# Seven products in place of eight for MLP2's gate and value, with its decoded weights staged through DRAM

## The chip, the cores and the metric

One core of a Trainium2 chip runs the kernel. The metric is the device time of one execution in microseconds, as the median of several runs. The core has a matrix engine (PE), whose weight loads the profile lists apart (PEld), a vector engine (DVE), an activation engine (ACT) and a general engine (POOL). SP issues most of the transfers; ACT can issue some too. On-chip memory is called SBUF, and PE writes its sums to PSUM.

## The reference

Three layers follow each other. The first is a chunked state-space attention over 4 x 8 x 768 tokens, whose output is reshaped to 3072 tokens of 256 numbers. The two others are the MLPs:

```
h = x @ w_in                                   # 256 -> 2048
g = where(h > 0, h, exp(min(h, 0)) - 1)
x = g @ w_out                                  # 2048 -> 256     (MLP1)
g = x @ w_gate                                 # 256 -> 1536
val = x @ w_val                                # 256 -> 1536
out = (g * (1 / (1 + exp(-g))) * val) @ w_out2 # 1536 -> 256     (MLP2)
```

All inputs are float32.

## The kernel before, in words

**Numbers.** PE multiplies in a short format (fp32r). So nearly every float32 operand is held as a high part and a low part: ACT copies the value into the short format (high), and DVE or POOL subtracts that from the value (low). One exact product is then three matmuls, high x high, low x high, high x low (`mm3`, line 547, which issues them at line 555).

**Blocks.** The 3072 tokens are six blocks of 512 (`BLOCKS`). MLP1 runs over 6 blocks x 16 slices `f` of 128 hidden numbers, MLP2 over 6 blocks x 12 slices. A pair (block, slice) is here called a slot. The loop at line 815 goes through 96 MLP1 slots and then 72 MLP2 slots. In each it issues the slot's input product, its activation, and the output product of the slot three back (`LAG`). The attention units of block b+1 are worked into the MLP1 slots of block b, at offsets written by hand (`OFF`, `OFF1`, `OFF8`), so block 5, the last, has none. Each engine runs what it is given in program order.

**MLP1's slot.** `m_a` is 6 matmuls into one of two banks `h`. ACT makes relu(-h) (line 577) and its exponential (line 582), DVE joins them with h (line 583, which frees the bank), `split` makes the high part on ACT (line 560) and the low part on POOL (line 561), and `m_c` is 6 matmuls (line 604). Block 0 has a cheaper form of `m_c` (line 596). `m_end` (line 610) writes the block's result to `x2`.

**MLP2's slot.** `s_a` (line 657) is 12 matmuls: for gate and for value, 2 halves of the 256 inputs x 3. ACT makes the sigmoid of the gate (line 671), DVE multiplies it by the gate (line 676) and by the value (line 677), both of which it reads from PSUM. `split` follows, on ACT and POOL. `s_c` (line 680) is 6 matmuls, 2 halves of the output x 3. So a slot has 18 matmuls of 128x512. `s_end` (line 692) copies a block's two outputs out, one on DVE (line 696) and one on ACT (line 698), and SP stores them (line 699). `s_x` (line 648) splits a block's `x2` into high and low (lines 653, 654).

**MLP2's weights.** They come as float64 words. `decode` (line 121) loads a piece (line 132), ACT makes a scaled copy of the upper words (line 138), and DVE makes three steps `d0`, `d1`, `d2` (lines 141, 144, 148). A slice has 768 columns: 256 gate, 256 value, 256 output. `load_w2` (line 618) takes them in pieces of 512 and 256, and `step_w2` (line 630) makes the steps one by one: three for every four slots of blocks 1 to 4 (`W2K`), which decodes 8 of the 12 slices into the buffer `w2e`, and two a slot in block 5, which decodes the other 4. `pair_w2` (line 638) makes the high part on ACT (line 642) and the low part on DVE (line 643), in block 5 for four slices and in the first slots of MLP2 for the rest. Then high and low stay in SBUF for all blocks.

**Other work that the prediction names.** In the attention, DVE's line 370 is a scan of 1024 columns, POOL's line 480 a product of 128 columns.

Of the kernel before, what the change touches and what calls it, by code (L numbers as in the profile page):

```python
# [67 lines left out]
def ssm_mlp_glu_kernel(ctx, tc, a, bcs, xbc, w1, w2, consts, out):  # L68
# [548 lines left out]

    def load_w2():

        f, j = parts[len(loaded)]  # L620
        if j == 0:
            V2[f] = w2e[:, f * 768:(f + 1) * 768] if f < NE else ph2["w2l"].tile([128, 768], F32, name=f"w2v{f}")
        v = V2[f]
        cs = slice(0, 512) if j == 0 else slice(512, 768)
        load, ex, steps = decode(w2.bitcast(U32)[f, :, 2 * cs.start:2 * cs.stop])
# [22 lines left out]
    def s_x(b):
        n = BLOCKS[b]
        pool = ph2["xs" if b % 2 == 0 else "w2h"]  # L650
        hi = pool.tile([128, 2, 512], F32R, tag="x2h", name="x2h")[:, :, :n]
        lo = pool.tile([128, 2, 512], F32R, tag="x2l", name="x2l")[:, :, :n]
        nc.scalar.activation(hi, x2[b], AF.Copy)
        nc.vector.tensor_tensor(lo, x2[b], hi.bitcast(F32), ALU.subtract)
        xs[b] = (hi, lo)

    def s_a(b, f):
        n = BLOCKS[b]
        res = []
        for nm in "gv":  # L660
            p = ph2["ps" if nm == "g" else "psv"].tile([128, 512], F32, tag="h" if nm == "g" else "v", name=nm, bufs=2 if nm == "g" else 3)[:, :n]
            wh, wl = W2[nm, f]
            mm3(p, [((wh[:, k], wl[:, k]), (xs[b][0][:, k], xs[b][1][:, k])) for k in range(2)], True, True)
            res.append(p)
        gps[b, f] = res

    def s_e1(b, f):
        n = BLOCKS[b]
        pg, pv = gps.pop((b, f))
        m = work.tile([128, 512], F32, tag="m", name="m2")[:, :n]  # L670
        nc.scalar.activation(m, pg, AF.Sigmoid)  # L671
        gt[b, f] = m, pg, pv

    def s_e1b(b, f):
        m, pg, pv = gt[b, f]
        nc.vector.tensor_tensor(m, m, pg, ALU.mult)  # L676
        nc.vector.tensor_tensor(m, m, pv, ALU.mult)  # L677
        gt[b, f] = m

    def s_c(b, f, half=None):  # L680
        n = BLOCKS[b]
        if f == 0:
            ops_[b] = [ph2["ps"].tile([128, 512], F32, tag=f"c{m}", name=f"o{m}")[:, :n] for m in range(2)]
        g = gt[b, f] if half == 0 else gt.pop((b, f))
        wh, wl = W2["o", f]
        for m in range(2):
            if half is not None and m != half:
                continue
            ms = slice(m * 128, (m + 1) * 128)
            mm3(ops_[b][m], [((wh[:, ms], wl[:, ms]), g)], f == 0, f == NF2 - 1)  # L690
# [222 lines left out]
```

## Time and profile before

| | us |
|---|---|
| median of 3 runs (632.03 to 632.95) | 632.71 |
| the profiled execution | 632.59 |
| its span, first to last instruction | 630.8 |

| engine | busy us | share of the span |
|---|---|---|
| PE | 616.5 | 98% |
| PEld | 490.3 | 78% |
| DVE | 369.1 | 59% |
| ACT | 316.4 | 50% |
| POOL | 317.8 | 50% |

The profiled execution is 1.8 us longer than its span, for what lies before the first and after the last instruction. Busy is the time in which at least one instruction of the engine ran; a matmul's 0.39 us overlaps the next one's, so PE's load is read from the distance of the starts. The granted TensorE clock is 1.000, full speed, over the whole span.

### The profile page before, as it was taken

The page shows a single profiled execution, that of the slowest core. Times are in us where ns is not written, and L with a number is a line of the kernel's source. Part 1 is how long each engine was busy: PE and PEld are TensorE (multiplying, and loading weights), DVE is VectorE, ACT ScalarE, POOL GpSimd, SP SyncE. Part 2 cuts the span into 40 slices and gives each one's busy share as a digit, 9 for nine tenths or more (in the row PEclk, how much of TensorE's full clock was granted, in tenths as well). Part 3 has the DMA queues.
Part 4 walks back from the last instruction along what each step waited for, and adds up shares of the span by engine and source line. Part 5 has one row for each costly group of instructions (what it writes and reads, how often), then busy time and mean ns, then how long its engine had stood idle before and what let it go on. Part 6 is the DMA issues. An engine that isn't in the chain of part 4 may idle for free.

```text
span 630.8 us, 9681 instructions
## 1 busy us (share of the span) xinstructions
PE 616.5 (98%) x3632; PEld 490.3 (78%) x3632; DVE 369.1 (59%) x574; ACT 316.4 (50%) x572; POOL 317.8 (50%) x269
## 2 busy tenths in 40 slices
PE   5899999999999999999999999999999999999997
PEld 4556667778888888778878888888888888888886
DVE  6898878998687767754664753433433343343332
ACT  1455667767677667657785533322323322332322
POOL 4443569998887878754553333233333322333332
PEclk9999999999999999999999999999999999999999
DMA  7588534444454454211300000000000000000000
GB/s 210 204 276 255 159 107 156 132 135 148 142 150 133 136 156 145 81 34 50 101 0 1 0 2 33 1 1 27 7 0 1 33 1 1 35 0 1 34 0 33
DMA packets 21014, 49.26 MB, mean 78 GB/s; under 512 B 3544, under 2 KB 5976, under 8 KB 20968
## 3 DMA queue, kind: packets, MB, share of 16 engines
q1 hardware_dynamic: 20664, 48.46, 24.5%
q8 instruction: 28, 0.46, 0.3%
q10 hardware_dynamic: 304, 0.19, 0.1%
q14 instruction: 18, 0.15, 0.1%
HBM read 45.40 MB, written 3.24 MB: 77 GB/s over the span
## 4 chain that ended last, share of the span: by engine, by line
PE 82%; DVE 4%; issue 1%; ACT 1%; POOL 1%; DMA 0%; SPq 0%; DVEq 0%
PE h L555 16%; PE o L555 16%; PE v L555 16%; PE g L555 16%; PE c L604 15%; PE cb L431 1%; PE y L508 1%; PE c L596 1%; DVE m L583 1%; PE y L504 1%; DVE zc L319 1%; DVE E L370 1%; DVE E L445 0%; POOL xb L392 0%; DVE wov L144 0%
## 5 line engine op out<-in xcount | busy, mean ns | idle before, releaser
L561 POOL TENSOR_TENSOR gl<-m,gh 128x512 fp32r<-128x512 f32 x152 | 204.8, 1348 | 248.9 <-ACT gh L560 248.9
L676 DVE TENSOR_TENSOR m<-m,g 128x512 f32<-128x512 f32 x72 | 49.5, 688 | 163.9 <-ACT m L671 163.9
L671 ACT ACTIVATE m<-g 128x512 f32<-128x512 f32 x72 | 43.1, 599 | 185.6 <-PE g L555 185.5
L583 DVE SCALAR_TENSOR_TENSOR m<-m,h 128x512 f32<-128x512 f32 x96 | 65.6, 683 | 60.1 <-ACT m L582 60.0
L560 ACT ACTIVATE gh<-m 128x512 fp32r<-128x512 f32 x152 | 94.9, 624 | 10.7 <-DVE m L583 9.7
L555 PE MATMUL h<-xh,wih 128*128 128x512 f32 x192 | 81.5, 424 | 2.3 <-DVE x L476 1.9
L577 ACT ACTIVATE m<-h 128x512 f32<-128x512 f32 x96 | 56.9, 592 | 49.1 <-PE h L555 45.9
L555 PE MATMUL h<-xh,wil 128*128 128x512 f32 x192 | 75.9, 395 | 0.0
L604 PE MATMUL c<-gh,woh 128*128 128x512 f32 x160 | 62.3, 390 | 0.0
L604 PE MATMUL c<-gh,wol 128*128 128x512 f32 x160 | 62.3, 389 | 0.0
L582 ACT ACTIVATE m<-m 128x512 f32<-128x512 f32 x96 | 59.8, 623 | 0.5
L555 PE MATMUL h<-xl,wih 128*128 128x512 f32 x192 | 59.8, 392 | 0.0
L555 PE MATMUL g<-x2h,w2h 128*128 128x512 f32 x144 | 56.0, 389 | 0.0
L555 PE MATMUL g<-x2h,w2l 128*128 128x512 f32 x144 | 56.0, 389 | 0.0
L555 PE MATMUL v<-x2h,w2h 128*128 128x512 f32 x144 | 56.0, 389 | 0.0
L555 PE MATMUL v<-x2h,w2l 128*128 128x512 f32 x144 | 56.0, 389 | 0.0
L555 PE MATMUL o<-gh,w2h 128*128 128x512 f32 x144 | 56.0, 389 | 0.0
L555 PE MATMUL o<-gh,w2l 128*128 128x512 f32 x144 | 56.0, 389 | 0.0
L555 PE MATMUL o<-gl,w2h 128*128 128x512 f32 x144 | 56.0, 389 | 0.0
L677 DVE TENSOR_TENSOR m<-m,v 128x512 f32<-128x512 f32 x72 | 49.5, 688 | 7.5
L604 PE MATMUL c<-gl,woh 128*128 128x512 f32 x160 | 50.9, 389 | 0.0
L555 PEld LDWEIGHTS h<-xh,wih 128*128 128x128 f32 x192 | 36.5, 190 | 15.4 <-DVE m L583 3.9
(144 smaller groups left out, 1076.2 us busy)
## 6 DMA issues: line engine op xcount, KB each, us to landing
abc<-ac SPq DMA_DIRECT2D x16, 512.0 KB
bcraw<-in_bcs SPq DMA_DIRECT2D x32, 256.0 KB
raw<-in_w SPq DMA_DIRECT2D x14, 512.0 KB
w2e<-in_w SPq DMA_DIRECT2D x14, 512.0 KB
xb<-in_xbc SPq DMA_DIRECT2D x18, 256.0 KB
raw<-in_w SPq DMA_DIRECT2D x12, 256.0 KB
out_y<-yo SPq DMA_DIRECT2D x12, 256.0 KB
x<-in_xbc SPq DMA_DIRECT2D x5, 256.0 KB
```

Of the source, the lines that this page charges most:

```text
L319: eng.tensor_tensor(u[z], u[raw], u[z].bitcast(F32), ALU.subtract)
L370: nc.vector.tensor_tensor_scan(u["E"].rearrange("p h q -> p (h q)"), u["abc"].rearrange("p h q -> p (h q)"), ident8.rearrange("p h q -> p ...
L555: nc.tensor.matmul(dst, lhsT=l, rhs=r, start=first and i == 0, stop=last and i == len(ops) - 1, **kw)
L560: nc.scalar.activation(hi, src, AF.Copy)
L561: lo_eng.tensor_tensor(lo, src, hi.bitcast(F32), ALU.subtract)
L577: nc.scalar.activation(m, h, AF.Relu, scale=-1.0)
L582: nc.scalar.activation(m, m, AF.Exp, scale=-1.0)
L583: nc.vector.scalar_tensor_tensor(m, m, -1.0, h, ALU.add, ALU.max)
L604: nc.tensor.matmul(cps[b][m], lhsT=w[:, m * 128:(m + 1) * 128], rhs=r, start=f == 0 and w is wh and r is gh, stop=f == NF1 - 1 and r is gl)
L671: nc.scalar.activation(m, pg, AF.Sigmoid)
L676: nc.vector.tensor_tensor(m, m, pg, ALU.mult)
L677: nc.vector.tensor_tensor(m, m, pv, ALU.mult)
```

## The change

**The product.** For one slice, the gate and value weights are a 2 x 2 arrangement (gate, value by the two halves of the inputs), and two neighbouring blocks give a 2 x 2 arrangement of `x2` (two halves of the inputs by two blocks). The product of the two takes eight products of 128x128 by 128x512. The change takes a form of Strassen's scheme with seven, over three pairs of blocks x 12 slices, 36 steps in all. It needs four sums of the weights (`w2_sums`, on POOL, 128 columns each), four differences of the inputs (`x_sum`, DVE for the first pair, POOL for the others), and sums of the products behind (`s_step`). A step has 7 x 3 matmuls for gate and value and 4 x 3 for the output (`s_o`), 33. The sigmoid and one multiplication become one `Silu` on ACT. PSUM has four banks `pa` to `pd` for the products, of which three take a second product on top of the first.

**The weights.** All 12 slices are decoded in whole pieces of 768 columns in blocks 2 to 4: 10 steps of DVE in block 2, 11 in block 3, 15 in block 4, none in blocks 1 and 5. Each slice is stored to DRAM by a transfer on ACT's queue, in one of three buffers by turns, and loaded again by SP when its turn comes: three slices in block 5, the others in the first pair's steps 0 to 8. There they get their sums on POOL (slice f at step f-3), their high parts on ACT and their low parts on DVE in two parts of 640 and 512 columns (step f-2).

**The order.** MLP1 no longer overlaps with MLP2's slots: step 0 begins behind slot 95, and holds the last three `m_c`. Steps have places (`a` to `d`, `o`) at which other work is hooked in.

The core of the diff:

```
-NHL = 4
+NHL = 3
...
-W2K = [0,0,1,2]
-W2N = 2
+W2K = [[0], [1,0,1,1,0,1,0,1,1,0,1,0,1,1,0,1], [1,0,1,1,0,1,1,0,1,1,0,1,1,0,1,1], [1,1,1,1]]
+NR = 3
+WS = 1152
+OPS = ["b11", "t2", "t3", "t1", "b21", "t4", "b22"]
...
     def load_w2():
...
+        f = len(loaded)
+        v, raw, e = w2e[:, f % NR * 768:][:, :768], w2e[:, NR * 768 + f % 2 * 1536:][:, :1536], w2e[:, NR * 768 + 3072:][:, :768]
+        load, ex, steps = decode(w2.bitcast(U32)[f], raw, e)
         load()
+        loaded.append(f)
+        def end():
+            steps[2](v)
+            spills.append([2, lambda: nc.scalar.dma_start(v2d[f], v)])
+        w2steps.extend([lambda: (ex(), steps[0](v)), lambda: steps[1](v), end])
...
+    def w2_load(f):
+        pool = ph2["w2l" if f < NHL or f % 2 else "w2h"]
+        v = V2[f] = pool.tile([128, WS], F32, tag="v2", name=f"v2_{f}")
+        nc.sync.dma_start(v[:, :768], v2d[f])
+    def w2_sums(f):
+        a11, a12, a22, s3, s1, s2, s4 = (V2[f][:, 128 * i:128 * i + 128] for i in (0, 1, 2, 5, 6, 7, 8))
+        nc.gpsimd.tensor_tensor(s1, s3, a22, ALU.add)
+        nc.gpsimd.tensor_tensor(s3, a11, s3, ALU.subtract)
+        nc.gpsimd.tensor_tensor(s2, s1, a11, ALU.subtract)
+        nc.gpsimd.tensor_tensor(s4, a12, s2, ALU.subtract)
+    cols = [slice(0, 640), slice(640, WS)]
...
+    def x_sum(p, nm, eng):
...
+        l, r = dict(t3=("b22", "b12"), t1=("b12", "b11"), t2=("b22", "t1"), t4=("b21", "t2"))[nm]
+        eng.tensor_tensor(x[nm], x[l], x[r], ALU.subtract)
...
+    def s_step(j, hooks):
+        p, f = divmod(j, NF2)
...
+        def g_split(j, i, m, eng):
+            hi, lo = [work.tile([128, 512], F32R, tag=f"g{z}", name=f"g{z}", bufs=LAG + 1) for z in "hl"]
+            nc.scalar.activation(hi, m, AF.Copy)
+            eng.tensor_tensor(lo, m, hi.bitcast(F32), ALU.subtract)
+            gt[j, i] = hi, lo
+        prod("a", 0, "b11", True)
+        prod("b", 7, "t2", True)
+        prod("d", 5, "t3", True)
+        prod("c", 6, "t1", True)
+        s1 = mtile("s1")
+        nc.scalar.activation(s1, ps["a"], AF.Copy)
+        if j:
+            g_split(j - 1, 1, V.pop(j - 1), nc.gpsimd)
...
+        nc.vector.tensor_tensor(u2, s1, ps["b"], ALU.add)
+        nc.vector.tensor_tensor(u3, u2, ps["d"], ALU.add)
+        nc.scalar.activation(s5, ps["c"], AF.Copy)
+        hook("a")
...
+        nc.vector.tensor_tensor(u3, u3, s5, ALU.add)
+        prod("a", 1, "b21", False)
+        prod("d", 2, "t4", False)
+        prod("c", 8, "b22", False)
+        m0 = mtile("m0")
+        nc.scalar.activation(m0, ps["a"], AF.Silu)
+        hook("b")
+        nc.vector.tensor_tensor(s1, u2, ps["d"], ALU.add)
+        nc.vector.tensor_tensor(u2, u2, ps["c"], ALU.add)
+        nc.vector.tensor_tensor(m0, m0, s1, ALU.mult)
+        m1 = mtile("m1")
+        nc.scalar.activation(m1, u2, AF.Silu)
+        g_split(j, 0, m0, nc.gpsimd)
+        hook("c")
+        nc.vector.tensor_tensor(m1, m1, u3, ALU.mult)
+        V[j] = m1
+        hook("o")
+        if j:
+            for i in range(2):
+                for m in range(2):
+                    s_o(j - 1, i, m)
...
+        if j == 3 * NF2 - 1:
+            g_split(j, 1, V.pop(j), nc.vector)
+            for i in range(2):
+                for m in range(2):
+                    s_o(j, i, m)
+                    s_end(p, i, m)
+        hook("d")
...
         for i in range(W2S, last_a):
-            at(late, i, step_w2, W2K[(i - BASE) % 4], NE)
-        for i in range(last_a + 1, last_a + 17):
-            at(late, i, step_w2, W2N, NF2)
+            at(late, i, step_w2, W2K[i // NF1 - 1][i % len(W2K[i // NF1 - 1])])
+        at(late, last_a, open_a)
...
+        hooks = {}
+        for f in range(NHL, NF2):
+            if f > NHL:
+                at(hooks, (f - 4, "d"), w2_load, f)
+            at(hooks, (f - 2, "a"), w2_hi, f, 0)
+            at(hooks, (f - 3, "a"), w2_sums, f)
+            at(hooks, (f - 2, "b"), w2_hi, f, 1)
+            at(hooks, (f - 2, "b"), w2_lo, f, 0)
+            at(hooks, (f - 2, "d"), w2_lo, f, 1)
+        for p in range(1, NB // 2):
+            e = p * NF2
+            for k, nm in enumerate(("t3", "t1", "t2", "t4")):
+                at(hooks, (e - 5 + k, "c"), x_sum, p, nm, nc.gpsimd)
+            for k, nm in enumerate(OPS):
+                i, h, l = [(e - 3, "b", "d"), (e - 2, "b", "d"), (e - 2, "c", "d"), (e - 1, "b", "d"), (e - 1, "b", "d"), (e - 1, "c", "d"), (e - 1, "c", "a")][k]
+                at(hooks, (i, h), x_hi, p, nm)
+                at(hooks, (i + (l == "a"), l), x_lo, p, nm, nc.gpsimd if nm == "t4" else nc.vector)
```

`x_hi` and `x_lo` make high and low parts of 512 columns, `w2_hi` and `w2_lo` those of the weights' parts `cols`. A block's two outputs are copied out as before, on DVE and ACT, in the second step of the next pair.

## Rows read from the trace of the kernel before

**Rows 1.** Busy time by stretch: us, then per engine busy us (instructions), clock, DMA.

```profile
88.90:144.70 55.80, 55.28 (x382) 43.86 (x382) 49.10 (x65) 41.03 (x79) 53.91 (x42) 1.00 0.44 137
144.70:195.30 50.60, 50.60 (x338) 41.08 (x337) 38.44 (x61) 35.37 (x68) 40.46 (x33) 1.00 0.46 142
195.30:245.80 50.50, 50.50 (x329) 40.86 (x328) 37.65 (x61) 35.27 (x68) 39.29 (x32) 1.00 0.47 141
245.80:293.90 48.10, 48.10 (x269) 38.73 (x268) 28.92 (x47) 32.47 (x63) 30.37 (x24) 1.00 0.18 63
293.90:341.70 47.80, 47.80 (x211) 39.09 (x210) 27.12 (x46) 34.20 (x63) 23.14 (x17) 1.00 0.17 50
341.70:626.90 285.20, 285.20 (x1260) 236.18 (x1258) 115.39 (x157) 91.92 (x158) 90.74 (x70) 1.00 0.03 10
```

**Rows 2.** The page's chain that ended last, shares of the span by engine.

```profile
PE 82%; DVE 4%; issue 1%; ACT 1%; POOL 1%; DMA 0%; SPq 0%; DVEq 0%
```

**Rows 3.** Timeline of PE in MLP2: start, duration, engine, line, operands; two slots' first matmuls.

```profile
500.58 0.39 PE L555 MATMUL g<-x2h,w2h 128*128 128x512 f32 x1
...
504.66 0.39 PE L555 MATMUL g<-x2h,w2h 128*128 128x512 f32 x1
```

**Rows 4.** Groups by line, 341.7 to 626.9 us: busy us, mean ns, idle before.

```profile
L561 POOL TENSOR_TENSOR gl<-m,gh 128x512 fp32r<-128x512 f32 x70 | 90.7, 1296 | 192.4 <-ACT gh L560 192.4
...
L677 DVE TENSOR_TENSOR m<-m,v 128x512 f32<-128x512 f32 x69 | 47.5, 688 | 7.2
L560 ACT ACTIVATE gh<-m 128x512 fp32r<-128x512 f32 x70 | 43.6, 624 | 1.0 <-DVE m L677 1.0
...
L671 ACT ACTIVATE m<-g 128x512 f32<-128x512 f32 x69 | 41.3, 599 | 180.9 <-PE g L555 180.8
```

**Rows 5.** Timeline of one MLP2 slot: from the gate's last matmuls to the multiplications.

```profile
615.73 0.62 PE L555 MATMUL g<-x2l,w2h 128*128 128x512 f32 x2
...
616.44 0.60 ACT L671 ACTIVATE m<-g 128x512 f32<-128x512 f32 x1 [2.96 <-PE g L555]
...
617.07 0.69 DVE L676 TENSOR_TENSOR m<-m,g 128x512 f32<-128x512 f32 x1 [2.60 <-ACT m L671]
...
617.86 0.69 DVE L677 TENSOR_TENSOR m<-m,v 128x512 f32<-128x512 f32 x1
```

**Rows 6.** Timeline of DVE and POOL where two instructions overlap, at two places.

```profile
310.06 2.11 POOL L561 TENSOR_TENSOR gl<-m,gh 128x512 fp32r<-128x512 f32 x1 [0.96 <-ACT gh L560]
310.06 0.95 DVE L643 TENSOR_TENSOR w2l<-w2e,w2h 128x768 fp32r<-128x768 f32 x1
...
348.42 1.30 POOL L561 TENSOR_TENSOR gl<-m,gh 128x512 fp32r<-128x512 f32 x1 [2.78 <-ACT gh L560]
...
349.19 1.34 DVE L643 TENSOR_TENSOR w2l<-w2e,w2h 128x768 fp32r<-128x768 f32 x1
```

**Rows 7.** Groups by line, 88.9 to 330 us: DVE's long scan, POOL's small product.

```profile
L370 DVE TENSOR_TENSOR_SCAN E<-abc,ident 128x1024 f32<-128x1024 f32 x15 | 34.9, 2324 | 0.0
...
L480 POOL TENSOR_TENSOR sbd<-x,con 128x128 f32<-128x128 f32 x15 | 7.4, 495 | 0.0
```

**Rows 8.** DVE's instructions on the weights' buffer alone: us, busy us (instructions), clock, DMA.

```profile
88.90:144.70 55.80, 11.69 (x12) 1.00 0.44 137
144.70:195.30 50.60, 6.49 (x12) 1.00 0.46 142
195.30:245.80 50.50, 6.13 (x12) 1.00 0.47 141
```

**Rows 9.** The chain in order of time: one attention unit's long input product.

```profile
166.75 1.58 PE h L555 x6
```

**Rows 10.** Issue of a transfer on ACT's queue; ACT's table load at MLP2's start.

```profile
0.74 0.58 ACTq L714 DMA_DIRECT2D w2e<-in_consts  x1
...
L671 ACT ACT_TABLE_LOAD  x1: 1283/1283/1283, 330.8 to 330.8; - x1
```

**Rows 11.** Timeline of the end: the last copy and the last stores' issue.

```profile
626.62 1.59 SPq L699 DMA_DIRECT2D out_y<-yo  x2
...
627.26 0.60 ACT L698 ACTIVATE yo<-o 128x512 f32<-128x512 f32 x1 [3.96 <-PE o L555]
```

More of the change, by code (lines that the diff above doesn't have):

```diff
@@ L46 @@
 EB = 1
-PW0 = 8
 WARM = 0
@@ L118, in ssm_mlp_glu_kernel, with decode @@
     top = low - H * R - NT // 16
-    def decode(src, raw=None):
+    def decode(src, raw=None, e=None):
         tot = src.shape[1] // 2
@@ L136, in ex @@
         def ex():
-            t["e"] = stg.tile([128, 512], F32, tag="e", name="e", bufs=EB)[:, :tot]
+            t["e"] = e if e is not None else stg.tile([128, 512], F32, tag="e", name="e", bufs=EB)[:, :tot]
             nc.scalar.activation(t["e"], t["hi"].bitcast(F32), AF.Copy, scale=REBIAS)
@@ L610, in m_end, with spill_w2, step_w2 @@
             nc.scalar.activation(x2[b][:, m, :], c[m], AF.Copy)
-    W2, V2, xs, gps, ops_ = {}, {}, {}, {}, {}
-    parts = [(f, j) for f in range(NF2) for j in range(2)]
-    loaded, w2steps = [], []
+    W2, V2, xs, ops_, V = {}, {}, {}, {}, {}
+    loaded, w2steps, spills = [], [], []
     def load_w2():
[L620 to L625, printed above, removed]
-        load()
-        loaded.append((f, j))
-        w2steps.extend([lambda: (ex(), steps[0](v[:, cs]))] + [lambda st=st: st(v[:, cs]) for st in steps[1:]])
-    def step_w2(n, upto):
+        f = len(loaded)
+        v, raw, e = w2e[:, f % NR * 768:][:, :768], w2e[:, NR * 768 + f % 2 * 1536:][:, :1536], w2e[:, NR * 768 + 3072:][:, :768]
+        load, ex, steps = decode(w2.bitcast(U32)[f], raw, e)
+        load()
+        loaded.append(f)
[3 more added lines that the diff above has]
+        w2steps.extend([lambda: (ex(), steps[0](v)), lambda: steps[1](v), end])
+    def spill_w2(now=False):
+        for z in list(spills):
+            z[0] -= 1
+            if now or z[0] <= 0:
+                z[1]()
+                spills.remove(z)
+    def step_w2(n):
+        spill_w2()
         for _ in range(n):
-            if len(loaded) < 2 * upto and len(w2steps) <= 3:
+            while len(loaded) < NF2 and len(w2steps) <= 3:
                 load_w2()
@@ L648, in s_x @@
[L648 to L681, printed above, removed]
-        if f == 0:
[L683 to L690, printed above, removed]
@@ new lines, in x_lo, with s_half, s_o @@
+    def x_lo(p, nm, eng):
+        hi, lo = xs[p, nm]
+        eng.tensor_tensor(lo, XT[p][nm], hi.bitcast(F32), ALU.subtract)
+    def s_half(j, i):
+        return (ident8.rearrange("p h q -> p (h q)"))[:, 512 * i:512 * i + 512]
+    def s_o(j, i, m):
+        p, f = divmod(j, NF2)
+        if f == 0:
+            ops_[p, i, m] = ph2["ps"].tile([128, 512], F32, tag="h" if i else f"c{m}", name=f"o{i}{m}", bufs=2 if i else None)
+        ms = slice(384 + m * 128, 384 + m * 128 + 128)
+        mm3(ops_[p, i, m], [([w[:, ms] for w in W2[f]], gt[j, i])], f == 0, f == NF2 - 1)
```

182 lines of the change are left out of this document (109 added, 73 removed).

## The prediction

> **What bounds the kernel now.** I read the busy time by stretch first, because shares of the whole span mix stages with different limits. PE is busy all through blocks 2 to 5 of MLP1 and through MLP2, and has 0.52 us without work in block 1 (55.28 of 55.80); in MLP2 DVE works 115 of 285 us, ACT 92, POOL 91 [rows 1]. The chain that ended last says the same: 82% of it is PE [rows 2]. But a busy PE may still be a slow one, so I take the distance of starts. One MLP2 slot follows the other after 504.66 - 500.58 = 4.08 us [rows 3], and a slot is 18 matmuls: 0.2267 us each. The whole stretch gives 285.2 / 1260 = 0.2263 us [rows 1]. So MLP2 is matmuls without a gap at the full clock, and only fewer matmuls make it shorter. In MLP1 DVE is the next engine: 88% of block 1, 76% and 75% of blocks 2 and 3, 60% of block 4 [rows 1].
>
> **Part 1, the matmuls.** A pair of slots has 36 matmuls now, a step 33, and the step has the same shapes. 36 steps x 3 x 0.2267 = **-24.5 us**. All of it lies on the path, since nothing else does. A step without waits is 33 x 0.2267 = 7.48 us; below, times count from its first matmul.
>
> **Part 2, what a step asks of the others.** DVE has 7 operations of 512 columns at 0.69 [rows 4] and about four handovers of 0.10 from one to a next that needs it (617.07 + 0.69 to 617.86 [rows 5]): 5.2 us. ACT has 6 at 0.60 to 0.62, 3.7 us; POOL two at 1.30, 2.6 us [rows 4]. All fit into 7.48. The one tight place is the second product into bank d: it may not start before DVE has read the first out of it (u3). A product's end is heard 0.48 us after its last matmul's start (that one starts at 615.73 + 0.23, ACT at 616.44 [rows 5]). So: a is ready at 0.45 + 0.48 = 0.93, ACT's copy ends at 1.53, u2 waits for b (1.61) and ends at 2.30, u3 runs 2.40 to 3.09. PE comes to d again after 15 matmuls, at 3.40: 0.31 us to spare. The other banks have more. The output matmuls of the step before start at 4.76 and need POOL's low part, made by 3.6, only at 6.57. Cost of a plain step: 0. The cover is that 0.31 us; anything that puts DVE further back than this PE feels at once.
>
> In the first pair the weights are made ready in the same steps. DVE gets low parts of 640 and 512 columns, 0.82 (half way between 0.69 for 512 and 0.95 for 768 [rows 4, 6]) and 0.69; POOL gets four sums of 128 columns, nearest row 0.495 each, 2.0 us [rows 7]. Alone DVE would have 6.7 us, POOL 4.6, ACT 3.7 and two copies of about 0.7. But they collide. Where a DVE operation with both inputs in SBUF and a POOL operation overlap, the later one is held: DVE's 0.95 and POOL's 1.30, started together, end after 0.95 and 2.11; DVE's, started 0.77 into POOL's 1.30, takes 1.34 [rows 6]. MLP2's two multiplications read PSUM and never met this: 0.69 always [rows 4]. The change makes five such DVE operations in these steps (the sum with s5, the two multiplications, two low parts). If the two engines take turns, steps 1 to 6 need 3 x 0.69 + 0.82 + 0.69 + 4.6 = 8.2 us, 0.7 too much; steps 7 and 8, with an input difference of 1.30 on POOL besides, 9.5, 2.0 too much; step 9, without sums but with that difference and one more low part on DVE, 8.2, 0.7 too much. Together 6 x 0.7 + 2 x 2.0 + 0.7 = 8.9 us. That is the upper end. The lower end is 0: POOL's results have 3 us to spare (3.6 against 6.57), and DVE's waits can fall where it idles. Rows 6 hold POOL once and DVE once, and only what holds DVE reaches PE, so I take half: **+4.4 us**. At the second change of pairs the weights are done; the same count there gives 3 x 0.69 + 2 x 0.69 + 3.9 = 7.4 us, which fits: 0.
>
> The Trainium skill, page SBUF — State Buffer, section Who interferes with whom, has the rule: of a DVE instruction with two SBUF inputs and a POOL instruction that reads SBUF the second to issue is blocked until the first is done. The first place of rows 6 agrees (2.11 is 0.81 + 1.30); in the second DVE loses 0.39 of the 0.53 us that POOL still had. The rule taken strictly gives the upper end, so it speaks against this change.
>
> **Part 3, the decoding in MLP1.** Blocks 1 to 4 now decode two slices each, block 5 four. DVE pays 6.5 and 6.1 us for two in blocks 2 and 3 and 11.7 in block 1, where POOL has hardly a gap [rows 1, 8]: 3.2 us a slice where it is undisturbed. A whole slice at once has the same columns in half the instructions; I take 3.2 for it too. Block 2 gets 10 of 36 steps, 3.33 slices, 10.7 us in place of 6.5, and DVE reaches 42.6 of 50.6 us, 84%. Block 3: 3.67 slices, 11.7 for 6.1, 86%. Block 4: 5 slices, 16.0 for about 6.1, 81%. Block 1 falls to 37.4 of 55.8. None passes block 1's 88% of now, where PE lost 0.52 us. Lower end: 0. Upper end: a unit's scan of 2.32 [rows 7] and a whole step (3.2 / 3 = 1.07) in front of the operation that frees the bank h, 3.4 us. That operation has 1.9 to spare: 4.08 us from a product's end to the next in the same bank (two slots of 12 x 0.2267, less 6 matmuls), less two ACT operations and one on DVE with their handovers, 2.2. So 1.5 us for each of the 12 units of blocks 2 to 4, 18 us. What a unit costs today is one input product of 1.58 us where 6 x 0.2267 = 1.36 [rows 9], 0.22. I am nearest to that row and take the same once more per unit: **+2.6**. Block 1's idle PE comes back: **-0.5**.
>
> ACT makes the scaled copies of 768 columns and issues 12 stores, 0.58 each [rows 10], 7 us over three blocks in which it idles 15 us each [rows 1]. A store is issued two slots after its last step, so ACT does not wait for DVE; were it late, relu and exponential would queue behind it. The stores and reloads move 12 x 0.39 x 2 = 9.4 MB more; the DMA share is at most 0.47 and 0.03 in MLP2 [rows 1]. SP gets 12 loads more, behind the attention's. A reload goes into a buffer that DVE has last read about 1.3 us into the step and takes about 0.39 MB / 142 GB/s = 2.8 us [rows 1]; POOL's sums wait for it until 4.1 or so, and POOL's next low part is not due before 7.7. The load of slice 4 must wait for MLP1's space, at the end of step 0; what waits behind it is POOL's sum and then its low part, with 3 us to spare. 0; without that cover about 2.
>
> **Part 4, the ends.** The table load of 1.28 us comes once, as now [rows 10], on ACT. At the end the last low part is made behind the last multiplication, about 9.4 us into step 35, when PE would want it at 9.3; then a copy and two stores as now [rows 11]. Block 5 exchanges its decoding for splits. **+0.3**, 0 to 2.
>
> **Sum.** -24.5 + 4.4 + 2.6 - 0.5 + 0.3 = -17.7. The profiled execution took 632.59 us, 0.1 below the median of the runs: 632.6 - 17.7 = **614.9 us**.
>
> **Rivals.**
> - Everything is covered: 632.6 - 24.5 - 0.5 = 607.6. For it: three engines at 32 to 40% of MLP2 [rows 1]. Against it: the 0.31 us. Chance 0.15.
> - The turns at the shared port are paid whole: 8.9 for 4.4, 619.4. For it: the first place of rows 6; against it: the second, and POOL's 3 us. Chance 0.15. (The skill's rule named above would have this.)
> - DVE becomes the bound of blocks 2 to 4: 18 for 2.6, 630.3. For it: block 1's 11.7 us for the same decoding, and whole steps twice as long; against it: one step a slot, and 81 to 86% only. Chance 0.09.
> - Slower: a loop closes over the steps. ACT's copy, u2, u3, the second products d and c, the sum behind them, its Silu and the high part behind that precede the next step's copy on ACT: 0.6 + 0.7 + 0.8 + 1.8 + 0.8 + 0.7 + 0.8 = 6.2 us, inside 7.48. POOL can hold two operations in it for 1.30 each: 8.8, 1.3 over, 36 x 1.3 = 47 us, so about 655. It decides from 0.68 us over a step, 1.96 of waits in each of the 36. Against it: POOL works 2.6 of 7.48 us in most steps. Chance 0.06.
> - The weights are not there when wanted, so the products saved become waits: a reload of 10 us in place of 2.8 would cost 2.5 in each of 9 steps, 22 us: 637. Against it: the idle DMA. Chance 0.03.
>
> **The numbers.** 0.52 is left for the forecast, 609 to 624: its lower end leaves Parts 2 and 3 nearly free, its upper end has the port paid whole and about 5 us more in MLP1. With the port's rival inside, most of the covered case from 608.5 on and a part of the DVE case, 608.5 to 624 holds 8 in 10. A measurement tells 0.2%, 1.3 us, from no change. Slower: the last two rivals, 0.09. Same: a sliver of the DVE case, 0.02. Faster: 0.89.
>
> **What would show it.** Starts of PE 0.2267 us apart and steps of 7.48 us from step 10 on; steps 1 to 9 at 7.5 to 9.5, with PE waiting for u3 there and DVE's two-input operations and POOL's stretched beside each other; blocks 2 to 4 up to 1 us longer each with DVE at 81 to 86%; no clock below full. Wrong: steps of over 7.6 us in the second and third pair (a loop), blocks 2 to 4 longer by over 2 us, or PE waiting for a weight.

## The result, and the profile after

After the change the kernel takes **621.32 us** (median of 4 runs, 620.54 to 622.1), beside 632.5 for the kernel before on the same chip: ratio 0.9823, 95% interval 0.9806 to 0.984. The forecast was 614.9, the range 608.5 to 624.0. The profiled execution took 621.05 us, its span 619.3. The gain is 632.59 - 621.05 = 11.5 us of one profiled execution against another; 17.7 were foreseen.

The page after: busy time by engine, and the chain that ended last [rows 2].

```profile
PE 596.2 (96%) x3524; PEld 469.7 (76%) x3524; DVE 468.5 (76%) x676; ACT 369.6 (60%) x659; POOL 365.0 (59%) x326
...
PE 62%; issue 10%; DVE 6%; POOL 5%; DMA 4%; ACT 1%; POOLq 0%; DVEq 0%; ACTq 0%
```

PE's share of the chain fell from 82% to 62%: something else now sets part of the end. Where, the busy time by stretch shows. Its columns are those of [rows 1]; the first four lines are MLP1's blocks 1 to 4, the next is block 5, the rest cuts MLP2 where its character changes.

```profile
88.73:143.42 54.69, 54.69 (x383) 44.20 (x383) 38.82 (x55) 39.86 (x75) 52.51 (x42) 1.00 0.39 121
143.42:193.92 50.50, 50.50 (x336) 40.79 (x335) 41.67 (x58) 36.01 (x67) 39.92 (x33) 1.00 0.59 181
193.92:244.41 50.49, 50.49 (x329) 40.89 (x328) 43.59 (x60) 36.87 (x67) 41.03 (x32) 1.00 0.66 201
244.41:293.83 49.42, 48.48 (x269) 38.71 (x269) 37.89 (x52) 34.51 (x63) 32.90 (x24) 1.00 0.39 129
293.83:331.00 37.17, 36.80 (x162) 30.15 (x161) 19.67 (x27) 29.29 (x55) 25.84 (x26) 1.00 0.11 32
331.00:437.00 106.00, 100.10 (x430) 79.68 (x429) 94.52 (x115) 60.48 (x105) 64.00 (x67) 1.00 0.10 31
437.00:510.00 73.00, 73.00 (x323) 60.22 (x322) 48.39 (x71) 35.61 (x62) 29.45 (x23) 1.00 0.04 15
510.00:530.00 20.00, 18.00 (x78) 14.12 (x77) 18.18 (x22) 10.76 (x19) 10.03 (x7) 1.00 0.01 1
```

MLP1 ends where it ended: block 4 at 293.83, before at 293.90. In MLP2 PE had no gap before; now it lacks 5.9 us in the first pair and 2.0 around the second change of pairs, and in just these stretches DVE is busy 89% and 91%. Between them, from 437 to 510 us, PE is full. PE's timeline says what it waits for. First its waits in three steps at the first change of pairs and in one at the second; then a plain step, from its first matmul over the second product into bank d to the next step's first matmul; then the last wait of the program.

```profile
405.12 0.50 PE L742 MATMUL pd<-x_t4h,w2h 128*128 128x512 f32 x1 [1.14 <-DVE ident L763]
...
415.06 0.50 PE L742 MATMUL pd<-x_t4h,w2h 128*128 128x512 f32 x1 [2.16 <-DVE ident L763]
...
423.88 0.51 PE L742 MATMUL pd<-x_t4h,w2h 128*128 128x512 f32 x1 [1.02 <-DVE ident L763]
...
516.63 0.50 PE L742 MATMUL pd<-x_t4h,w2h 128*128 128x512 f32 x1 [1.10 <-DVE ident L763]
...
544.66 0.39 PE L742 MATMUL pa<-x_b11h,w2h 128*128 128x512 f32 x1
...
548.06 0.39 PE L742 MATMUL pd<-x_t4h,w2h 128*128 128x512 f32 x1
...
552.14 0.39 PE L742 MATMUL pa<-x_b11h,w2h 128*128 128x512 f32 x1
...
612.95 0.50 PE L556 MATMUL o<-gl,w2h 128*128 128x512 f32 x1 [0.35 <-POOL gl L750]
```

A plain step is 552.14 - 544.66 = 7.48 us, and PE comes to bank d 3.40 after the step's start: both as worked out ahead. PE has eight waits at that place, all for u3 (the instruction at line 763), and none anywhere in MLP2 for a weight; four of the reloads, not three, are issued before MLP2 begins, the last eight from step 0 on. Numbering the steps 0 to 35, the starts give:

| steps | us each | above 7.48 in all |
|---|---|---|
| 0 | 8.84 (39 matmuls, no wait) | 0 |
| 1 to 8 | 7.48 to 8.13 | 2.3 |
| 9 to 13 | 8.92, 9.96, 8.83, 8.80, 7.72 | 6.8 |
| 23, 24 | 8.88, 8.85 | 2.8 |
| all others | 7.48 | 0 |

So 11.9 us of the 24.5 went back. By the distances of PE's starts 11.5 of them fall at the second product into bank d, in waits for u3; the profile counts 7.8 as idle time, because a matmul's 0.39 us outlasts the 0.23 to the next start. Why u3 is late is seen on DVE and POOL between steps 10 and 11 (step 11 starts at 419.30); the last three lines are the same places in a plain step, which starts at 552.14.

```profile
418.31 0.69 DVE L784 TENSOR_TENSOR m<-m,ident 128x512 f32<-128x512 f32 x1 [0.15 <-ACT m L781]
418.92 1.82 DVE L708 TENSOR_TENSOR x_t2o<-x,x_t2o 128x512 fp32r<-128x512 f32 x1
420.65 1.78 DVE L708 TENSOR_TENSOR x_t3o<-x,x_t3o 128x512 fp32r<-128x512 f32 x1
422.36 0.68 DVE L762 TENSOR_TENSOR ident<-s,pb 128x512 f32<-128x512 f32 x1
...
418.90 1.29 POOL L750 TENSOR_TENSOR gl<-m,gh 128x512 fp32r<-128x512 f32 x1 [4.14 <-ACT gh L749]
420.14 1.74 POOL L689 TENSOR_TENSOR x<-x 128x512 f32<-128x512 f32 x1
...
551.18 0.69 DVE L784 TENSOR_TENSOR m<-m,ident 128x512 f32<-128x512 f32 x1 [0.15 <-ACT m L781]
...
553.76 0.69 DVE L762 TENSOR_TENSOR ident<-s,pb 128x512 f32<-128x512 f32 x1 [1.89 <-PE pb L742]
...
551.77 1.29 POOL L750 TENSOR_TENSOR gl<-m,gh 128x512 fp32r<-128x512 f32 x1 [3.75 <-ACT gh L749]
```

What the prediction calls the shared port is at work in these lines: a DVE instruction with both inputs in SBUF and a POOL instruction hold each other up. DVE finishes the second multiplication (m1, line 784) and takes the low part of an input. POOL began its own low part (gl) 0.02 us earlier, and DVE's instruction lasts 1.82 instead of 0.69. The next one is held by POOL's input sum in the same way. Behind both stands u2 (line 762): it starts 422.36 - 419.30 = 3.06 us into the step, in a plain step 553.76 - 552.14 = 1.62. That is 1.44 late where 0.31 were to spare, so 1.13 reach PE; the step is 1.35 longer, and the other 0.2 comes with the stop itself (the first matmul behind it lasts 0.50 instead of 0.39, for one). The reading that the experiments test: what hurts is not the number of these instructions but that two held ones stand in front of the operation with the least slack.

The Trainium skill, page SBUF — State Buffer, section Who interferes with whom, has it that the second of such a pair to issue is blocked until the first is done. The trace agrees on who is held; DVE lost 1.82 - 0.69 = 1.13 us of the 1.27 that gl still had to run. At a lead as small as this one the traces do not always agree (next section).

### The profile page after: what moved, and what is told of

Its sections match the earlier page's. It is cut to its first block, busy times and chain, and to the rows that moved or that the text cites. A ratio compares the mean times of both kernels' runs of the same rounds, so it can differ in the third digit from the quotient of the medians.

```text
span 619.3 us, 9832 instructions
## 1 busy us (share of the span) xinstructions
PE 596.2 (96%) x3524; PEld 469.7 (76%) x3524; DVE 468.5 (76%) x676; ACT 369.6 (60%) x659; POOL 365.0 (59%) x326
## 4 chain that ended last, share of the span: by engine, by line
PE 62%; issue 10%; DVE 6%; POOL 5%; DMA 4%; ACT 1%; POOLq 0%; DVEq 0%; ACTq 0%
PE h L556 16%; PE c L605 15%; PE o L556 10%; PE pd L742 5%; POOL gl L750 5%; PE pa L742 5%; PE pc L742 4%; DMA w2e<-in_w 4%; PE pb L742 3%; PE cb L432 1%; PE y L509 1%; PE c L597 1%; DVE w2l L670 1%; DVE ident L763 1%; DVE ident L762 1%
## 5 line engine op out<-in xcount | busy, mean ns | idle before, releaser
L781 ACT ACTIVATE m<-ident 128x512 f32<-128x512 f32 x36 | 22.8, 633 | 61.4 <-DVE ident L778 61.4
L762 DVE TENSOR_TENSOR ident<-s,pb 128x512 f32<-128x512 f32 x36 | 24.6, 683 | 40.4 <-PE pb L742 36.6
L393 POOL TENSOR_TENSOR xb<-xb,P 128x128 f32<-128x128 f32 x16 | 38.0, 2374 | 14.2 <-DVE P L387 14.2
L764 ACT ACTIVATE x<-pc 128x512 f32<-128x512 f32 x36 | 21.5, 598 | 35.3 <-PE pc L742 35.3
L556 PEld LDWEIGHTS h<-xl,wih 128*128 128x128 f32 x192 | 36.5, 190 | 8.0
```

The source lines that it names most:

```text
L393: nc.gpsimd.tensor_tensor(u["ct"], u["ct"], u["P"], ALU.mult)
L556: nc.tensor.matmul(dst, lhsT=l, rhs=r, start=first and i == 0, stop=last and i == len(ops) - 1, **kw)
L762: nc.vector.tensor_tensor(u2, s1, ps["b"], ALU.add)
```

## The experiments

Theory: DVE's low parts are issued just behind m1, when POOL has just got its input, so DVE is the one held, and u2 stands behind it. Rivals: the number of such instructions in a step (in any order); POOL's weight sums; and, for MLP1's share, the staging. Each expectation was written ahead of its run. Edits 1 to 3 and 5 to 8 are made in the changed kernel; the kernel before took 632.2 to 632.6 us beside each. Two things repeat only roughly from one trace to another. Block 5's first matmul starts anywhere from 284.3 to 287.6 us in the traces of the changed kernel and of runs 1 to 3 and 5 to 9, which share the program up to there; and who is held is partly chance. Over the steps of the eleven traces of kernels with seven products there are 91 places where gl and a 512-column low part of DVE start within 0.06 us of each other. With POOL 0.03 to 0.06 ahead DVE was held in all 41; with POOL 0 to 0.02 ahead DVE was held in 36 and POOL in 14. That alone moves a step by up to a microsecond with no edit near it, so single steps prove little.

**1. The low parts of three inputs later.** Those of b11, t2 and t3, from the end of their steps to the middle of the next:

```diff
-i, h, l = [(e - 3, "b", "d"), (e - 2, "b", "d"), (e - 2, "c", "d"), ...
+i, h, l = [(e - 3, "b", "n"), (e - 2, "b", "n"), (e - 2, "c", "n"), ...
-at(hooks, (i + (l == "a"), l), x_lo, ...
+at(hooks, (i + (l in "an"), "b" if l == "n" else l), x_lo, ...
```

> The low parts of the inputs b11, t2, t3 for the next pair move from the end of steps 9, 10 (and 21, 22), where they stand in front of u2 on DVE, to the middle of the step behind, before s1. Same operations, same amount. Theory H (what costs is that POOL holds DVE at the end of a step, in front of u2, which has only 0.31 us to spare): step 10 falls from 9.96 to about 8.2 us, steps 11 and 23 from 8.83 and 8.88 to 7.5 to 7.9; steps 9, 12 and 24 stay; in all -3.5 to -4.5, about 617.3 us. Rival L (DVE has too much to do in these steps, in whatever order): steps 9 to 12 keep their sum, at most -1, 620.5 us or more.

Measured: 619.27 us (618.51 to 621.71), ratio 0.9795 (0.977 to 0.9819): 2 us less, not 3.5 to 4.5. Steps 10, 11 and 23 fell from 9.96, 8.83 and 8.88 to 8.27, 7.48 and 7.48. But steps 12 and 24 rose from 8.80 and 8.85 to 10.64 and 10.17. DVE and POOL at the start of step 12, and what PE waits for there:

```profile
425.24 1.83 DVE L708 TENSOR_TENSOR x_t1l<-x,x_t1h 128x512 fp32r<-128x512 f32 x1
426.99 1.76 DVE L708 TENSOR_TENSOR x_b21l<-x,x_b21h 128x512 fp32r<-128x512 f32 x1
...
427.12 0.50 PE L742 MATMUL pc<-x_t1l,w2h 128*128 128x512 f32 x1 [0.69 <-DVE x_t1l L708]
...
428.81 0.50 PE L742 MATMUL pa<-x_b21l,w2h 128*128 128x512 f32 x1 [0.72 <-DVE x_b21l L708]
```

These two low parts stayed in the old place. They were held in the changed kernel too (1.83 and 1.78), but there the first began 0.4 us before step 12; here step 11 is 1.35 shorter, it begins 1.5 us into the step, and PE waits for the low parts themselves. The three that moved are no longer held (0.68 each). In the middle of step 11 DVE's sum with s5 is now held, 1.36 for 0.69, and the step still takes 7.48: a held instruction that is out of u2's way costs nothing. The last two cannot go later, since PE wants them within the first 3.2 us of the next step.

**2. POOL's input sums earlier.** The four differences for the next pair move off the steps that make the low parts (into block 5 for the second pair, five steps earlier for the third):

```diff
-at(hooks, (e - 5 + k, "c"), x_sum, p, nm, nc.gpsimd)
+if p == 1:
+    at(late, last_a + 10 + k, x_sum, p, nm, nc.gpsimd)
+else:
+    at(hooks, (e - 10 + k, "c"), x_sum, p, nm, nc.gpsimd)
```

> POOL's four input differences for the second pair move into MLP1's block 5, those for the third pair from steps 19 to 22 to steps 14 to 17. DVE's work in the steps around the change of pairs stays as it is. Theory H: the second of two low parts at a step's end is no longer held by a difference (1.78 us falls to about 0.7), so steps 10, 11 and 23 get shorter by about 1 us each: -2.5 to -3.5, about 618.3 us; the first low part stays at 1.82, held by the step's own gl. Rival L: POOL's work is not DVE's, 0 to -0.5.

Measured: 615.26 us (614.23 to 615.46), ratio 0.9726 (0.971 to 0.9742): 6 us less, about twice what was expected. The steps are 6.0 above 7.48 in all instead of 11.9: step 10 fell to 8.08, step 11 to 7.68, step 23 to 7.75; steps 12 and 24, where POOL makes t4's low part, stayed at 8.79 and 8.80. Some 1.7 us of the gain lie in steps 1 to 9, which the expectation did not name. In steps 10, 11 and 23 one held instruction instead of two stands in front of u2, and 0.31 us of it is free each time (for step 11 it is the second, 1.78, while the first ran at 0.68).

**3. No weight sums on POOL.** Left out for slices 3 to 11, whose columns a load fills:

```diff
+        if f >= NHL:
+            nc.sync.dma_start(v[:, 768:], v2d[f][:, :384])
...
-            at(hooks, (f - 3, "a"), w2_sums, f)
```

> Leaves out POOL's sums of the weights for slices 3 to 11 (the columns are filled by a small transfer instead), so the gate and value products of those slices are not the reference's. Theory H: steps 1 to 8 took 2.3 us over 7.48 each in all, and what POOL's sums held of DVE's middle low part and its sum with s5 goes: -1 to -2.3, steps 1 to 8 at 7.5 to 7.6, about 619.5 us. Rival: steps 1 to 8 are long because of the 512-column low part that gl holds at the step's end; then they stay between 7.5 and 8.1 and the time moves by less than 0.7.

Measured in a single execution: 619.36 us. The time is the theory's, but not by its way. Steps 1 to 8 are still 1.8 above 7.48 (2.3 with the sums), much as the rival has it. Most of the 2 us is in steps that hold no sums: steps 9 and 11 fell to 8.22 and 7.66, step 12 rose to 9.26, steps 10 and 24 are unchanged (9.98, 8.80). The trace shows chance at work: where DVE's low part was held, 1.8 us, in steps 2, 4, 6 and 8, they took 7.80 to 8.20 (only step 3 kept 7.48); in steps 5, 7 and 11 POOL was held instead, and they took 7.48, 7.48 and 7.66. So the sums, 2.0 us a step in the forecast's count, cost some 0.5 us over steps 1 to 8 together, if anything.

**4. The staging alone.** In the kernel before: whole slices decoded in blocks 2 to 4, stored on ACT's queue, reloaded, with MLP2 and its order as they were.

```diff
-W2K = [0,0,1,2]
+W2K = [[0], [1,0,1,1,0,1,0,1,1,0,1,0,1,1,0,1], [1,0,1,1,0,1,1,0,1,1,0,1,1,0,1,1], [1,1,1,1]]
...
+            spills.append([2, lambda: nc.scalar.dma_start(v2d[f], v)])
...
+        nc.sync.dma_start(v, v2d[f])
```

> The kernel before with the change's decoding alone: whole slices in blocks 2 to 4, stored to DRAM on ACT's queue, loaded again by SP; MLP2 with its old slots of 18 matmuls. The prediction's terms for this were +2.6 - 0.5 = +2.1, 634.6 us. The trace of the changed kernel, whose block 4 ends within 0.1 us of the old one's, says 0: 632.5 us, within 0.7. Rival: the reloads are late in MLP2's first slots, +1 to +3.

Measured: 632.24 us (631.68 to 633.1, 10 runs), ratio 0.9997 (0.9988 to 1.0006). Nothing, as a sum: block 1, without decoding, is about 1.1 us shorter and block 4 longer by 1.7 (49.81 for 48.10).

**5. One weight low part ahead of m1.** A change of order within a step, no operation more or less:

```diff
-            at(hooks, (f - 2, "d"), w2_lo, f, 1)
+            at(hooks, (f - 2, "c"), w2_lo, f, 1)
```

> One low part of the weights (512 columns, slice f, step f-2) moves from behind m1 to in front of it on DVE, nothing else. There it begins before POOL's gl(j, 0), which waits for ACT's high part. Theory H (who begins later is held, and 0.02 us decide): the low part takes 0.69 in place of 1.82, POOL is held instead and has time; steps 2 to 8 go from 2.3 us over in all to under 0.7, and steps 9 and 10, which begin behind such a low part, get shorter by about 1 us each: -3 to -4, about 618 us. Rival (the two engines' sum at the port is what counts): the wait only changes its owner, steps 2 to 10 keep their length, within 0.7 us.

Measured: 617.75 us (617.04 to 620.03), ratio 0.9771 (0.9746 to 0.9797). The same place in step 2, first in the changed kernel, then here:

```profile
346.35 1.82 DVE L670 TENSOR_TENSOR w2l<-v,w2h 128x512 fp32r<-128x512 f32 x1
...
346.33 1.29 POOL L750 TENSOR_TENSOR gl<-m,gh 128x512 fp32r<-128x512 f32 x1 [1.87 <-ACT gh L749]
```

```profile
345.70 0.69 DVE L670 TENSOR_TENSOR w2l<-v,w2h 128x512 fp32r<-128x512 f32 x1
346.30 0.68 DVE L784 TENSOR_TENSOR m<-m,ident 128x512 f32<-128x512 f32 x1
```

The low part falls from 1.82 to 0.69 and steps 1 to 8 to 7.47 to 7.49: their 2.3 us are gone although the same instructions run. Step 9 fell from 8.92 to 7.67 and step 11 from 8.83 to 7.89; step 10, which was to get shorter, rose to 11.22, of which the last section tells.

**6. t4's low part on DVE instead of POOL**, at the start of steps 12 and 24.

```diff
-i, h, l = [..., (e - 1, "c", "d"), (e - 1, "c", "a")][k]
+i, h, l = [..., (e - 1, "c", "a"), (e - 1, "c", "a")][k]
-at(hooks, (i + (l == "a"), l), x_lo, p, nm, nc.gpsimd if nm == "t4" else nc.vector)
+at(hooks, (i + (l == "a"), l), x_lo, p, nm, nc.vector)
```

> The low part of the input t4 at a change of pairs goes from POOL (end of step 11, 23) to DVE (step 12, 24, behind u3). POOL does less, DVE more. Theory H: the low part of b21 in front of u2 is no longer held by it (1.78 to 0.69), steps 12 and 24 get shorter by about 1.0 each: -2, about 619.3 us. Rival L (DVE has too much to do there): steps 12 and 24 get longer by up to 0.6 each: +1.

Measured: 618.93 us (618.01 to 619.76), ratio 0.9783 (0.9766 to 0.9799). Steps 12, 23 and 24 fell from 8.80, 8.88 and 8.85 to 7.91, 7.86 and 8.23; steps 10 and 11 did not move (9.96, 8.82). Step 12 fell as expected: the low part of b21 takes 0.68, with that of t1 held as before (1.82). The fall of step 23 is not the edit's, and that of step 24 not its alone: there chance had POOL held, as in step 23:

```profile
511.85 0.68 DVE L708 TENSOR_TENSOR x_t2l<-x,x_t2h 128x512 fp32r<-128x512 f32 x1
...
511.83 1.85 POOL L750 TENSOR_TENSOR gl<-m,gh 128x512 fp32r<-128x512 f32 x1 [3.28 <-ACT gh L749]
```

One operation more on the busier engine, and step 12 gets shorter: the load of DVE is not the matter.

**7. The input low parts ahead of m1.** As 5, for five of the six inputs whose low part DVE makes at a change of pairs; the high part of one of them, t3, also moves one place ahead on ACT.

```diff
-i, h, l = [(e - 3, "b", "d"), (e - 2, "b", "d"), (e - 2, "c", "d"), (e - 1, "b", "d"), (e - 1, "b", "d"), ...
+i, h, l = [(e - 3, "b", "c"), (e - 2, "b", "c"), (e - 2, "b", "c"), (e - 1, "b", "c"), (e - 1, "b", "c"), ...
```

> Only the order of two DVE operations at each change of pairs is turned: the low part of an input (both inputs in SBUF) is issued ahead of the second gated multiplication instead of behind it, its high part on ACT one hook earlier; t4's stays on POOL. Theory (who is issued second at the shared port is held, and only what holds DVE in front of u2 reaches PE): the low parts take 0.7 us instead of 1.8, POOL's g low part 1.6 instead of 1.3; steps 9, 10, 11 fall from 8.9, 10.0, 8.8 to 8.2 to 9.0 each, step 23 from 8.9 to 7.5 to 7.8, steps 12, 13 and 24, with t4 on POOL, stay: 3 us less, about 618.3. Rival (the count of two-input operations in a step sets it, in whatever order): steps unchanged, 621.3.

Measured: 615.71 us (615.58 to 616.56), ratio 0.9739 (0.9725 to 0.9754): 5.6 us less for order alone, where 3 were expected. DVE and POOL between steps 10 and 11 again (step 11 starts at 417.35):

```profile
416.52 0.68 DVE L708 TENSOR_TENSOR x_t2o<-x,x_t2o 128x512 fp32r<-128x512 f32 x1
417.13 0.68 DVE L708 TENSOR_TENSOR x_t3o<-x,x_t3o 128x512 fp32r<-128x512 f32 x1
417.73 1.78 DVE L784 TENSOR_TENSOR m<-m,ident 128x512 f32<-128x512 f32 x1
419.43 0.67 DVE L762 TENSOR_TENSOR ident<-s,pb 128x512 f32<-128x512 f32 x1
...
417.35 1.61 POOL L750 TENSOR_TENSOR gl<-m,gh 128x512 fp32r<-128x512 f32 x1 [3.28 <-ACT gh L749]
```

Now DVE is first and POOL's gl is held, 1.61 for 1.29, which POOL can afford. One hold of DVE is left, of m1, and u2 starts 2.08 into the step instead of 3.06. Steps 9 to 11 take 8.26, 8.60 and 7.81, steps 23 and 24 take 7.51 and 8.22. Steps 12 and 24, which were to stay at 8.8, fell too, step 12 to 8.27. The rival that counts instructions is out.

**8. More slack for u3.** The first product into bank c is made twice in every step, 3 matmuls more, so that PE comes to bank d 0.68 us later:

```diff
         prod("c", 6, "t1", True)
+        prod("c", 6, "t1", True)
```

> The first product into bank c is made twice in every step (the second time from zero again, so the values are the same): 3 matmuls of 0.2267 us more, 0.68 us a step, 24.5 us in 36 steps, and PE comes to bank d 0.68 us later, so that u3 has 0.99 us to spare instead of 0.31. Theory (plain steps are bound by PE; what stretched the others was DVE's lateness beyond u3's 0.31 us): plain steps 8.16; steps 1 to 8 over that by 0 to 0.1 each, steps 9 to 13, 23 and 24 over by 0.2 to 1.8 each where they were over by 0.2 to 2.5; 24.5 less about 6, so about 640. Rival (the held time at the port is paid in whatever slack): 621.3 + 24.5 = 645.8. Rival (plain steps are bound by the loop over DVE, ACT and POOL, not by PE): steps stay near 7.5 and the time below 630.

Measured: 637.96 us (635.45 to 639.11), 16.6 us more than the changed kernel for 24.5 us of matmuls. The longer of its two waits for u3 (the extra line makes u3's line 764), then the first matmuls of two plain steps that follow each other:

```profile
433.69 0.50 PE L742 MATMUL pd<-x_t4h,w2h 128*128 128x512 f32 x1 [0.66 <-DVE ident L764]
...
561.03 0.39 PE L742 MATMUL pa<-x_b11h,w2h 128*128 128x512 f32 x1
...
569.19 0.39 PE L742 MATMUL pa<-x_b11h,w2h 128*128 128x512 f32 x1
```

Plain steps take 8.16, exactly the 36 matmuls, so PE is what bounds them. Steps 1 to 8 take 8.16 too, also those where DVE was held for 1.8 us (3, 6, 7 and 8); only steps 10, 12 and 23 are over it by more than 0.1, by 0.43, 0.95 and 0.71, 2.2 us in all where the changed kernel has 11.9. So holds at the port are paid only beyond u3's slack, and the rival that has them paid in whatever slack is out. The trace is of the fastest of the four executions, 635.45 us, 14.4 above the changed kernel's traced one; the three others took 2 to 3.7 us more, which no trace explains.

**9. All together.** Edits 2 and 5, the low parts of 7 ahead of m1, and t4's low part on DVE.

> All low parts of inputs and weights that stood at a step's end now stand in front of m1, t4's goes to DVE behind u3, and POOL's input differences are made early (as in the run with them early, 615.3 us, whose steps were 6.0 us over in all). Theory H: 1 to 3 us over are left: 610.5 to 612.5 us. Rival: steps 12 and 24 must make the low parts of t1, b21, t4 and b22 between the last use in one step and the first use in the next, whatever the order, and stay at 8.8: then 613 to 615 us.

Measured: 612.05 us (611.1 to 612.87), ratio 0.9674 (0.9659 to 0.9688). All steps are 7.48 to 7.50 except 10, 12 and 24 (8.16, 8.20, 8.22); 2.2 us of the 11.9 are left. Steps 12 and 24 are not at the rival's 8.8; what is left in them is PE's wait for t4's low part.

**10. and 11. The decoding spread otherwise, on top of 9.** First evenly over blocks 1 to 4, then 12 steps in each of blocks 2 to 4 (9 has 10, 11 and 15):

```diff
+W2K = [[1,0,1,0,1,0,1,0,1,0,1,1,1,0,1,0]] * 4
```

> The combined kernel with the decoding spread evenly: 9 steps of a whole slice's decoding in each of blocks 1 to 4 instead of 0, 10, 11 and 15. Theory (block 4's 1.3 us more than before the change comes from its 15 whole steps, and block 1's 1.1 us less from having none): block 1 back from 54.7 to 55.2 to 55.8, block 4 from 50.0 to 48.1 to 49.0, so 612.0 again within 1 us. Rival (block 4's extra is a raw weight load that comes late, whatever DVE does): block 4 stays at 49 to 50 and the sum is 613.

```diff
+W2K = [[0], [1,0,1,1] * 4, [1,0,1,1] * 4, [1,1,1,0]]
```

> The combined kernel with 12 steps of a whole slice's decoding in each of blocks 2, 3 and 4 instead of 10, 11 and 15, and none in block 1. Theory (block 4's 1.3 to 1.9 us more than the 48.1 of before come from its 15 steps, blocks 2 and 3 have room): block 4 at 48.1 to 49.0, blocks 2 and 3 at 50.5 as before, block 1 at 54.7; 611.0, 1 us less. Rival (12 steps are already too many in blocks 2 and 3, where DVE has the more other work): these grow by 0.5 or more each and the sum stays at 612.0 or rises.

Measured: 612.91 us (612.67 to 613.13) and 610.27 us (609.88 to 610.6), ratios 0.9692 (0.9678 to 0.9706) and 0.9646 (0.9632 to 0.9659). Busy time by stretch: blocks 1 and 4 with the even spread, then blocks 3 and 4 with 12 steps each.

```profile
88.49:146.10 57.61, 55.48 (x381) 43.77 (x381) 50.72 (x62) 41.46 (x77) 55.94 (x42) 1.00 0.55 167
...
247.23:295.36 48.13, 48.13 (x269) 38.76 (x269) 33.11 (x46) 32.66 (x61) 29.94 (x24) 1.00 0.24 83
```

```profile
194.06:244.93 50.87, 50.70 (x329) 40.94 (x328) 47.32 (x61) 36.78 (x67) 41.34 (x32) 1.00 0.69 203
244.93:293.06 48.13, 48.13 (x269) 38.73 (x269) 35.72 (x49) 33.53 (x62) 32.66 (x24) 1.00 0.33 107
```

Block 4 is back at 48.13 in both. In block 1 nine steps cost 57.61 - 54.69 = 2.9 us; in block 3, 12 steps cost 0.4 with DVE at 93%. The last one is the fastest kernel of this study, 11 us below the changed one, by order and placing alone. What lengthens block 4 with 15 steps is a raw load that ACT waits for. Its wait in block 4 of the changed kernel, then two scaled copies that follow each other there and in the last run:

```profile
ACT w2e L137 <- DMA w2e<-in_w: 2.2, 1, 2.2
```

```profile
248.45 0.91 ACT L137 ACTIVATE w2e<-w2e 128x768 f32<-128x768 f32 x1
...
259.28 0.92 ACT L137 ACTIVATE w2e<-w2e 128x768 f32<-128x768 f32 x1 [2.20 <-DMA w2e<-in_w]
```

```profile
250.50 0.90 ACT L137 ACTIVATE w2e<-w2e 128x768 f32<-128x768 f32 x1
...
262.98 0.91 ACT L137 ACTIVATE w2e<-w2e 128x768 f32<-128x768 f32 x1
```

With 15 steps ACT wants the next raw slice 8.6 us after the last copy, with 12 only after 12.5, and then the load has landed. The ten traces with 15 steps in block 4 (the changed kernel, runs 1 to 9) have that wait, from 1.5 to 3.6 us, and nine of them agree that block 4, from its first product to block 5's, is 48.9 us plus the wait, to 0.05 us; it was 49.8 before the change. The tenth, run 6, is 1.0 longer than that, and there the clock fell (last section). So both the theory and the rival of run 10 have a part: the load is late, and it is late because the steps ask for it sooner.

## Why the forecast was right in direction and 6 us too low

- **Part 1 held.** -24.5 us: 21 steps take 7.48 and run 8 shows that matmuls set them. No loop, no late weight; those two rivals fell. Yet one of the prediction's signs of being wrong is there: steps 12, 13, 23 and 24, in the second and third pair, take 7.72 to 8.88 us, over 7.6. It is not the loop that the sign was meant for, but Part 2.
- **The weak point held.** u3 with 0.31 us to spare, before PE's second product into bank d, was named; all eight long waits are there.
- **Part 2's sum failed: +11.9 for +4.4.** For steps 1 to 9 the sum was close, 2.3 + 1.4 = 3.7 for 4.4, but by luck: 1.0 (half of 2.0) was forecast for each of steps 7 and 8, which gave 0.36 and 0, and 0.35 for step 9, which gave 1.44; and run 3 shows that the weight sums, on which the count rests, cost little. The step that failed is "at the second change of pairs the weights are done; the same count there gives ... 7.4 us, which fits: 0". There 2.8 was measured, and the like steps 10 to 13 of the first change, at 0 too, gave 5.4. A count of what the port must carry in a step says nothing of where in the step it falls. The runs show that order decides: the same instructions ahead of m1 cost 5.6 us less (run 7) and steps 1 to 8 nothing (run 5); in neither trace was there a place where chance had POOL held. In the terms of the forecast: "DVE's waits can fall where it idles" was true of the middle of a step and false of its end, where u2 stands behind; and "POOL's results have 3 us to spare" was right, but in the order of this change DVE is the first to be held.
- **The rival "the port paid whole", 619.4,** came nearest in microseconds, yet its places were wrong: its 8.9 us all lay in steps 1 to 9, 3.7 of them came, and 8.2 came from steps it had at 0.
- **Part 3: 0 for +2.1.** No unit of MLP1 pays 0.22 more: blocks 2 and 3 take 50.50 and 50.49 (before 50.60 and 50.50) with DVE at 83% and 86%. The 0.22 from which the term was taken is in the changed kernel as it was: a unit's first product still takes 1.58 us. Block 1 gave back 1.1, not 0.5, and block 4 took 1.3, for a late raw load (0.6 to 3.7 in the ten traces with 15 steps there). Run 4 has the sum by itself: 0.9997.
- **Part 4:** PE waits 0.35 us in step 35 (612.95 above), not for the last low part, as foreseen, but for POOL's before it, which ends at 612.90; DVE makes the last one by 613.44, a microsecond before its use. The product behind the wait starts 0.5 and the last matmul 0.64 later than at an even distance; +0.3 was foreseen. Block 5's stretch lacks 37.17 - 36.80 = 0.4 us of PE.

Together: -24.5 + 11.9 - 0.1 + 0.4 + 0.6 = -11.7, measured -11.5. The forecast's -17.7 is off by +7.5 in Part 2, -2.2 in Part 3 and +0.7 in the ends. That Part 3 was too high made the whole miss smaller than Part 2's; that is luck.

## What to carry to other kernels

Before adding work to an engine that looks idle, find the operation with the least slack in its queue and see what will stand directly in front of it; a busy share, or a sum over a step, does not show that. Where instructions of two engines hold each other up, as 1.82 us for 0.69 shows here, arrange the order so that the one with slack comes second, and clearly so: here that is DVE's two-input operations before the moment when POOL gets its input. Work that only shares the port, like the input sums (run 2), belongs in steps where no two-input operation of DVE stands in front of one without slack.

## What the runs showed of the hardware that was not expected

- A lead of 0.02 us does not settle who is held, other than run 5's expectation had it. In the changed kernel gl began at 418.90, DVE's low part at 418.92, and DVE paid 1.13 us; in run 6 they began at 511.83 and 511.85, DVE ran at 0.68 and gl took 1.85 for 1.29. From 0.03 us on the first one won in all 41 places. With DVE's low part 0.22 ahead (run 7, 417.13 to 417.35) it ran at 0.68 and gl paid 0.3.
- A wait of PE can cost more than itself. In run 5, PE waited 1.84 us in step 10, and shortly after that the granted clock fell. PE's timeline, then the busy time from 412 to 416 us:

```profile
411.37 0.50 PE L742 MATMUL pd<-x_t4h,w2h 128*128 128x512 f32 x1 [1.84 <-DVE ident L763]
...
412.33 0.63 PE L742 MATMUL pc<-x_b22h,w2h 128*128 128x512 f32 x1
412.75 0.63 PE L742 MATMUL pc<-x_b22h,w2l 128*128 128x512 f32 x1
```

```profile
412.00:416.00 4.00, 4.00 (x12) 3.13 (x11) 3.44 (x6) 1.37 (x3) 0.42 (x2) 0.58 0.00 0
```

The starts are 0.42 apart instead of 0.227, the lower of the two clock levels (1.2 of 2.4 GHz), for 8 matmuls: 8 x 0.2 = 1.6 us of the step's 11.22. In run 6 the same came in block 4 (granted clock 0.57 from 264 to 268 us), behind a wait of PE of 1.8 us. In the changed kernel the wait of 2.16 in step 10 was not followed by that; why the one and not the other stays open.
- A raw load of 768 KB issued at 247.19 us landed 12.01 us later, in block 4, where the DMA share is 0.39. In the ten traces with 15 steps there the copy that waits for this load starts 11.3 to 13.5 us behind its issue. What the load stands behind was not tried.
